# Loads by token halves, contiguous 32x32 turns of rows, and batch 0's query products turned by TensorE for a two-head block matrix, in a new order

## The chip, the cores and the metric

One core of one Trainium2 chip. The metric is the device time of one execution in microseconds (us). Before: a median of 122.04 us over 3 runs (122.0 to 123.68).

## What is computed

Attention with a polynomial sketch, then a small residual network on its output. Cut to what matters:

```python
# q, k, v: (4 batches, 4 heads, 1088 tokens, 32); S1, S2: (8, 32)
def phi(x):                                   # 64 features of a token
    a = np.einsum('rd,bhsd->bhsr', S1, x)
    b = np.einsum('rd,bhsd->bhsr', S2, x)
    return np.einsum('bhsi,bhsj->bhsij', a, b).reshape(*x.shape[:-1], 64)
kv = np.einsum('bhsf,bhsd->bhfd', phi(k), v)
z = np.sum(phi(k), axis=2)
attn = np.einsum('bhsf,bhfd->bhsd', phi(q), kv) / (phi(q) . z + 1e-6)
x = attn.transpose(0, 2, 1, 3).reshape(4, 1088, 128)
xn = (x - mean(x)) / sqrt(var(x) + 1e-6) * g_ln
out = x + relu(xn @ w_ch1) @ w_ch2            # w_ch1 (128, 512), w_ch2 (512, 128)
```

S1, S2 and the two weights arrive as 64-bit words and are turned into float32 on the chip by bit operations (`w_ex` ... `w_mul`, L279 to L341).

## The kernel before

Everything is float32. The four batches go one after another through the attention; each batch gives two chunks of 512 tokens (chunk c = 2b and 2b+1, four tiles of 128) and a rest of 64 tokens, and two rests make the chunks 8 and 9 (one tile each). Each chunk then goes through the network.

**Keys of a batch.** `ld k` brings rows (a partition holds 34 tokens), `turn_g`/`turn_r` (L419, L435) turn them in 32x32 blocks on DVE into kT. Features come in one of two ways: `k_dir` (L461) multiplies nine token tiles of kT with `sk0` and leaves features by token in PSUM, which ACT copies (`k_cp`); or `k_feat` (L478) makes eight small matmuls and `k_tok` (L489) turns their result on DVE. Batches 0 and 1 use the first way, 2 and 3 the second. Then products on POOL or DVE (`k_prod`, `k_prod0`), the sums `k_sum`, `k_zs`, `k_sc`, and `k_val` (72 records on PE) into KV.

**Queries.** Batch 0 is loaded token by token (`ld_t`, `ld_tr`, L149 to L160, runs of 128 bytes) and turned by PE (`turn_p`, L442) with copies on ACT; the others are loaded as rows and turned by DVE. `q_dir` (batch 0) or `q_feat`/`q_tok` give features; `q_ac`, `q_den`, `q_rec`, `q_a2`/`q_b0` make the denominator and scale one factor; `q_prod` makes the 64 products per head and token; `q_turn` (L648) turns them in 32x32 blocks on DVE into qpT; `num` (L656) contracts them with kvr in 32 small matmuls per call (64 records), and `num_cp` copies the result to xT, the chunk by feature.

**Network of a chunk.** `hid` (L770) gives 128 hidden units for 512 tokens in one matmul, `relu` moves them to hT, `sec` (L785) makes one tile of 128 tokens in four matmuls. A chunk's rows for the residual and the statistics come by PE (`row_pe`, chunks 0, 1, 8, 9) or through DRAM (2 to 7): `row_turn` (DVE, L723), `row_wr`, `row_rd` (two DMAs, L729 and L735). `st_bn`, `st_ag` (L748) and `st_pow` (POOL, L756) give the scale, `fin` (DVE) or `fin_a`/`fin_g` (ACT, POOL) the output, `store` the DMA.

PSUM is six tiles: X0 and X1 (two banks each: the letters A, B and C, D of the program), M0 (M), M1 (N), PO (O) and KV (K). The order of everything on every engine is one hand-set table of operations, `PROGRAM` (L840); the framework puts the semaphores between engines by tile, so that a wait may be for a later use of the other half of the same tile. A DMA on SP or ACT is an instruction in that engine's queue; it also waits there until an earlier DMA that used the same of eight semaphores has landed. `fill` (L252) are matmuls on ones that keep PE busy in the opening.

Of the kernel before, what the change touches and what calls it, by code (L numbers as in the profile page):

```python
# [25 lines left out]
def kernel(  # L26
# [121 lines left out]
    @op  # L148
    def ld_t(eng, h, u0, u1):  # L149
        by[eng].dma_start(  # L150
            out=_ap(qt, 0, P, P * u0 + D * h, [[P, u1 - u0], [1, D]]),
            in_=bass.AP(q.tensor, q.offset + (h * S + u0) * D, [[8 * D, P], [D, u1 - u0], [1, D]]),
        )
# [23 lines left out]
    ident8 = const([R, P], F32, "ident8")  # L177
# [264 lines left out]
    def turn_p(z, u0, u1):  # L442
        for u in range(u0, u1):
            n = P if u < 8 else 64
            pe.transpose(banks[z][:, P * (u - u0) : P * (u - u0) + n],
                         qt[0:n, P * u : P * (u + 1)], ident[0:n, 0:n])
# [276 lines left out]
    def row_turn(c):  # L723
        n = tiles(c)
        dve.transpose(_ap(xh[slot(c)], 0, P, 0, [[32 * n, 4], [32, n], [1, 32]]),  # L725
                      _ap(cols(c), 0, P, 0, [[1, 4], [P, n], [4, 32]]))
# [225 lines left out]
```

## Time and profile before

| | |
|---|---|
| median of 3 runs | 122.04 us |
| the profiled execution | 122.71 us, its span 120.9 us |
| PE busy | 108.4 us (90%) |
| DVE busy | 84.0 us (69%) |
| POOL, ACT busy | 48.4 us (40%), 38.7 us (32%) |
| DMA | 15502 packets, 13.31 MB; 6528 packets under 512 bytes |

The span runs from the first to the last recorded instruction; what lies around it (1.81 us in this execution) is start and end of the program. PE is the matmuls, PEld the weight loads beside them; every float32 matmul gives two records. Rows of the timeline read: start, duration of the piece, engine, line, operation, tiles, count, and in brackets the idle time before and what ended it. ACTq and SPq are DMA issues in those engines' queues.

### The profile page before, as it was taken

The page shows a single profiled execution, that of the slowest core. Times are in us where ns is not written, and L with a number is a line of the kernel's source. Part 1 is how long each engine was busy: PE and PEld are TensorE (multiplying, and loading weights), DVE is VectorE, ACT ScalarE, POOL GpSimd, SP SyncE. Part 2 cuts the span into 40 slices and gives each one's busy share as a digit, 9 for nine tenths or more (in the row PEclk, how much of TensorE's full clock was granted, in tenths as well). Part 3 has the DMA queues.
Part 4 walks back from the last instruction along what each step waited for, and adds up shares of the span by engine and source line. Part 5 has one row for each costly group of instructions (what it writes and reads, how often), then busy time and mean ns, then how long its engine had stood idle before and what let it go on. Part 6 is the DMA issues. An engine that isn't in the chain of part 4 may idle for free.

```text
span 120.9 us, 3295 instructions
## 1 busy us (share of the span) xinstructions
PE 108.4 (90%) x1347; PEld 78.6 (65%) x1347; DVE 84.0 (69%) x229; ACT 38.7 (32%) x100; POOL 48.4 (40%) x64
## 2 busy tenths in 40 slices
PE   5993999999898998998999799999979979979970
PEld 3382999848766773874665589766237946549970
DVE  2953308249999799899788999885993655391550
ACT  0062124224334358030701820264491500414000
POOL 6502242035839963301587903339643500006100
PEclk9999999999999999999999999999999999999997
DMA  3999799996000023011640120013640225300423
GB/s 110 262 315 245 139 251 233 272 249 182 0 5 5 0 62 131 0 26 68 203 147 0 43 87 0 5 66 118 188 159 0 87 92 173 91 17 13 161 87 108
DMA packets 15502, 13.31 MB, mean 110 GB/s; under 512 B 6528, under 2 KB 12416, under 8 KB 15488
## 3 DMA queue, kind: packets, MB, share of 16 engines
q1 hardware_dynamic: 11744, 9.54, 28.5%
q10 hardware_dynamic: 3712, 3.57, 9.7%
q8 instruction: 10, 0.16, 0.6%
q14 instruction: 4, 0.03, 0.1%
q0 software_dynamic: 32, 0.00, 0.0%
HBM read 9.31 MB, written 3.80 MB: 108 GB/s over the span
## 4 chain that ended last, share of the span: by engine, by line
PE 57%; DVE 18%; DMA 8%; ACT 6%; issue 4%; POOL 2%; ACTq 1%; DVEq 0%; POOLq 0%
PE X L772 8%; PE M L788 7%; PE X L663 5%; PE M L772 5%; DMA kn<-in_k_dram 4%; PE X L788 4%; DVE xh L725 4%; PE KV L788 3%; PE X L463 3%; DVE qpT L649 3%; DMA w_raw<-in_moe_w_ch_dram 3%; PE PO L788 3%; PE PO L772 2%; ACT xT L82 2%; PE M L463 2%
## 5 line engine op out<-in xcount | busy, mean ns | idle before, releaser
L758 POOL TENSOR_TENSOR rstd<-va,mhalf 128x4 f32<-128x4 f32 (+1 forms) x10 | 10.2, 1024 | 29.1 <-DVE va L752 28.1
L788 PEld LDWEIGHTS M<-w,hT 128*128 128x128 f32 x144 | 17.1, 192 | 5.1 <-issue 2.4
L788 PE MATMUL M<-w,hT 128*128 128x128 f32 x144 | 18.4, 278 | 1.1 <-ACT ob L807 0.6
L772 PE MATMUL X<-xT,w 128*128 128x512 f32 (+1 forms) x38 | 18.4, 586 | 0.8 <-DVE xr L84 0.8
L780 ACT ACTIVATE hT<-X 128x512 f32<-128x512 f32 (+2 forms) x18 | 9.9, 556 | 21.3 <-PE X L772 19.8
L87 POOL TENSOR_TENSOR kp<-kf 128x1280 f32<-128x1280 f32 (+3 forms) x7 | 13.1, 1883 | 4.9 <-ACT kf L82 3.2
L87 POOL TENSOR_TENSOR qp<-a,fq 128x1280 f32<-128x1280 f32 (+1 forms) x4 | 9.6, 2398 | 5.1 <-DVE a L87 5.0
L649 DVE STREAM_TRANSPOSE qpT<-qp 128x1280 f32<-128x1280 f32 (+2 forms) x9 | 11.0, 1227 | 0.5 <-POOL qp L87 0.4
L82 ACT COPY xT<-X 128x256 f32<-128x256 f32 (+1 forms) x13 | 6.1, 510 | 15.9 <-PE X L663 11.5
L772 PE MATMUL M<-xT,w 128*128 128x512 f32 (+1 forms) x20 | 9.0, 532 | 1.4 <-DVE hT L782 0.9
L254 PE MATMUL M<-ones 128*128 128x128 f32 (+2 forms) x16 | 8.7, 696 | 1.4 <-DVE m L202 1.4
L772 PEld LDWEIGHTS X<-xT,w 128*128 128x128 f32 x38 | 6.3, 190 | 4.7 <-issue 4.2
L663 PE MATMUL X<-qpT,kvr 32*32 32x288 f32 (+2 forms) x384 | 7.9, 332 | 1.1 <-issue 0.5
L725 DVE STREAM_TRANSPOSE xh<-xT 128x512 f32<-128x512 f32 x6 | 6.5, 1102 | 0.9 <-ACT xT L82 0.9
L772 PEld LDWEIGHTS M<-xT,w 128*128 128x128 f32 x20 | 3.4, 189 | 5.5 <-issue 1.9
L663 PEld LDWEIGHTS X<-qpT,kvr 32*32 32x32 f32 x384 | 4.7, 103 | 3.0 <-issue 1.0
L745 DVE BATCH_NORM_STATS2 st<-x 128x6 f32<-128x128 f32 x32 | 6.7, 274 | 0.0
L788 PEld LDWEIGHTS X<-w,hT 128*128 128x128 f32 x48 | 5.9, 192 | 1.0 <-issue 1.0
L788 PEld LDWEIGHTS KV<-w,hT 128*128 128x128 f32 x40 | 4.9, 191 | 2.2 <-ACT hT L780 1.7
L788 PE MATMUL X<-w,hT 128*128 128x128 f32 x48 | 6.2, 275 | 0.0
L772 PE MATMUL PO<-xT,w 128*128 128x512 f32 (+1 forms) x14 | 6.2, 522 | 0.0
L817 POOL TENSOR_TENSOR ob<-ob,x 128x512 f32<-128x512 f32 x4 | 5.1, 1282 | 2.5 <-ACT ob L807 2.5
(164 smaller groups left out, 195.2 us busy)
## 6 DMA issues: line engine op xcount, KB each, us to landing
out_dram<-ob SPq DMA_DIRECT2D x7, 256.0 KB, 2.9
vn<-in_v_dram SPq DMA_DIRECT2D x13, 128.0 KB, 4.8
qn<-in_q_dram SPq DMA_DIRECT2D x3, 544.0 KB, 5.6
xd<-xh SPq DMA_DIRECT2D x5, 256.0 KB, 2.3
kn<-in_k_dram ACTq DMA_DIRECT2D x2, 544.0 KB, 6.3
x<-xd SPq DMA_DIRECT2D x4, 256.0 KB, 2.7
kn<-in_k_dram SPq DMA_DIRECT2D x1, 544.0 KB, 7.5
w_raw<-in_moe_w_ch_dram SPq DMA_DIRECT2D x1, 512.0 KB, 6.3
```

What stands on the lines that cost most here:

```text
L82: act.copy(o, i)
L87: by[eng].tensor_tensor(out=o, in0=a, in1=b, op=ALU.mult)
L254: pe.matmul(M[0][:, 0:w], ones[:, 0:P], ones[:, 0:w], start=True, stop=True)
L463: pe.matmul(banks[z][:, KW * (u - u0) : KW * (u - u0 + 1)], kT[b % 2][:, P * u : P * (u + 1)], sk0, start=True, stop=True)
L649: dve.transpose(_ap(qpT, 0, P, 32 * u0, [[32, u1 - u0], [TW, 8], [1, 32]]), qp[:, H * F * u0 : H * F * u1])
L663: pe.matmul(XS[r // 2][D * h : D * h + D, o : o + w], kvr[b % 2][rows, DM * f + D * h : DM * f + D * h + D], qpT[rows, c : c + w], start=( ...
L725: dve.transpose(_ap(xh[slot(c)], 0, P, 0, [[32 * n, 4], [32, n], [1, 32]]), _ap(cols(c), 0, P, 0, [[1, 4], [P, n], [4, 32]]))
L745: dve.bn_stats(out=sts[slot(c)][:, 6 * t : 6 * t + 6], in_=row_ap(c, t))
L758: pool.tensor_tensor(out=rstds[slot(c)][:, 0:n], in0=vas[slot(c)][:, 0:n], in1=mhalf[:, 0:n], op=ALU.pow)
L772: pe.matmul(banks[z][:, 0:n], w1[:, P * j : P * (j + 1)], cols(c)[:, a : a + n], start=True, stop=True)
L780: act.activation(o, i, AF.Relu)
L788: pe.matmul(banks[z][:, DM * t : DM * (t + 1)], h[:, 512 * j + P * t : 512 * j + P * (t + 1)], w2[:, DM * j : DM * (j + 1)], start=(j == 0 ...
```

## The change

* **Loads.** S1 and S2 are stacked on 16 partitions instead of side by side on 8 (`s_raw`, `s_f`, `ident8`); one matmul `sk` gives both columns, and the broadcast for `s2b` becomes an own step, `sk_b`. Batch 0's queries are loaded as rows like the others, in two parts (`ld_h` and `ld`), and turned on DVE by a new `turn_h` (16 tokens of each row, contiguous), which also takes the place of `turn_g` for all queries. `ld_t`, `ld_tr`, `turn_p`, `turn_c` are gone. All early loads but one are issued by SP; ACT issues a single small one.
* **Batch 1's keys** go by `k_feat` and `k_tok` instead of `k_dir` and three copies.
* **Batch 0's numerator.** `q_turn` and `num` are replaced, for batch 0 only, by `q_flip` (PE transposes of 128x128, 18 in all), `q_flcp` (copies of these from PSUM) and `num0`: kv is laid out as a block matrix of two heads (`k_vcp0`, `k_spr0`, `k_rcp0`, kvb cleared by `c_kvb`), and two matmuls per call, each 128 features by 64 outputs, do what 32 small ones did.
* **Rows.** `row_turn` reads a chunk contiguously and writes 32-blocks apart; `row_rd` becomes four DMAs of 32 partitions each; `store` and `store_r` have one layout for all batches.
* **Statistics.** The addition of 1e-6 moves from DVE (`st_ag`) to POOL (`st_pow`).
* **Order.** The whole table is new, with other engines for many copies, relus and products.

The diff, cut to its core:

```diff
-    s_raw = const([R, 2 * D], S1.dtype, "s_raw")
+    s_raw = const([2 * R, D], S1.dtype, "s_raw")
-    qt = const([P, H * TW], F32, "qt")
-    qn = [qt] + const([P, G * D], F32, "qn", B - 1)
+    qn = const([P, G * D], F32, "qn", B)
...
+    def ld_h(eng, x, b, half):
+        ld(eng, x, b, 16 * half, 16 * half + 16)
...
     def sk():
-        for i in range(2):
-            pe.matmul(KV[:, 64 + R * i : 64 + R * (i + 1)], s_f[:, DM * i : DM * (i + 1)],
-                      ident[0:R, 0:R], start=True, stop=True)
-        pe.matmul(KV[:, 80 : 80 + D], ident8, s_f[:, DM : DM + D], start=True, stop=True)
+        pe.matmul(KV[:, 64 : 64 + 2 * R], s_f, ident[0 : 2 * R, 0 : 2 * R], start=True, stop=True)
+    def sk_b():
+        pe.matmul(KV[:, 80 : 80 + D], ident8, s_f[:, 0:D], start=True, stop=True)
...
+    def turn_h(x, b, half):
+        dst, src = turned[x]
+        dve.transpose(
+            _ap(dst[b % 2], 0, P, P * 4 * half, [[32, 4], [P, 4], [1, 32]]),
+            src[b][:, 512 * half : 512 * half + 512],
+        )
...
+    def k_vcp0(eng):
+        copy(eng, _ap(kvc, 0, P, 0, [[F, 2], [1, F]]), _ap(KV, 0, P, 0, [[0, 2], [1, F]]))
+    def k_spr0():
+        pe.transpose(KV[:, 256:384], kvc[:, 0:P], ident)
+    def k_rcp0(eng):
+        for i in range(2):
+            copy(eng, _ap(kvb, 64 * i, 64, 32 * i, [[64, 2], [1, 32]]),
+                 _ap(KV, 64 * i, 64, 256 + 32 * i, [[64, 2], [1, 32]]))
+    def q_flip(u0, u1, p, z):
+        for u in range(u0, u1):
+            pe.transpose(banks[z][:, P * (u - u0) : P * (u - u0 + 1)],
+                         qp[:, 2 * P * u + P * p : 2 * P * u + P * (p + 1)], ident)
+    def q_flcp(eng, u0, u1, p, z):
+        copy(eng, qpT[:, NU * P * p + P * u0 : NU * P * p + P * u1], banks[z][:, 0 : P * (u1 - u0)])
+    def num0(u0, u1, z):
+        for p in range(2):
+            pe.matmul(banks[z][64 * p : 64 * p + 64, 0 : P * (u1 - u0)], kvb[:, 64 * p : 64 * p + 64],
+                      qpT[:, NU * P * p + P * u0 : NU * P * p + P * u1], start=True, stop=True,
+                      tile_position=(0, 64 * p))
...
     def row_turn(c):
         n = tiles(c)
-        dve.transpose(_ap(xh[slot(c)], 0, P, 0, [[32 * n, 4], [32, n], [1, 32]]),
-                      _ap(cols(c), 0, P, 0, [[1, 4], [P, n], [4, 32]]))
+        dve.transpose(_ap(xh[slot(c)], 0, P, 0, [[32, n], [32 * n, 4], [1, 32]]), cols(c))
...
-    def row_rd(eng, c):
+    def row_rd(eng, c, r):
         w = D * tiles(c)
         by[eng].dma_start(
-            out=rows_of(c).rearrange("p (h w) -> p h w", h=H),
-            in_=bass.AP(xd[c].tensor, xd[c].offset, [[w, P], [P * w, H], [1, w]]),
+            out=_ap(rows_of(c), 32 * r, 32, 0, [[w, H], [1, w]]),
+            in_=bass.AP(xd[c].tensor, xd[c].offset + w * r, [[P // 32 * w, 32], [P * w, H], [1, w]]),
         )
...
-        dve.tensor_tensor(out=vas[slot(c)][:, 0:n], in0=_ap(mv, 0, P, 1, [[2, n]]),
-                          in1=eps[:, 0:n], op=ALU.add)
...
     def st_pow(c):
         n = tiles(c)
+        pool.tensor_scalar(out=vas[slot(c)][:, 0:n], in0=_ap(mvs[slot(c)], 0, P, 1, [[2, n]]),
+                           scalar1=1e-6, scalar2=None, op0=ALU.add)
...
     PROGRAM = """
-    c_ones; fill 1 128; ld_g; ld_s S 1; c_pads 1; c_small; c_pads 0; c_vpad 1; c_iota; c_ident;
+    c_ones; fill 1 256; fill 2 512; c_ident; c_iota; ld_s A 1; c_pads 0; ld_g; c_vpad 1;
```

Three places of the order are used by the prediction. Names are tiles (kf features of keys, qt/qp queries and their products, X_65 and X_66 the two-bank PSUM tiles).

ACT from its first instruction to the first copy of key features, before:

```order
L118 DMA kn_73<-in_k_dram 128x512
L165 DMA w_raw<-in_moe_w_ch_dram 128x256
L118 DMA kn_73<-in_k_dram 128x576
L118 DMA kn_74<-in_k_dram 128x1088
L150 DMA qt<-in_q_dram 128x4x32
L206 ACT_TABLE_LOAD
L206 ACTIVATE warm<-one 128x1
L292 ACTIVATE exf_122<-ex_121,m_96 128x256
L150 DMA qt<-in_q_dram 128x4x32
L308 ACTIVATE low_124<-w_raw 128x256
L408 COPY skq_110<-KV 128x16
```

and of the change:

```order
L108 DMA s_raw<-in_S_dram 8x32
L194 ACT_TABLE_LOAD
L194 ACTIVATE warm<-one 128x1
L297 ACTIVATE mant_117<-bits_114,one 16x32
L297 ACTIVATE mant_122<-bits_119,one 128x256
L289 ACTIVATE exf_121<-ex_120,m_95 128x256
L406 COPY skq_109<-KV 128x16
L305 ACTIVATE low_123<-w_raw 128x256
```

Six DMA issues ahead of the copy of the sketch (skq) have become one, and that copy now stands ahead of the weights' low words.

PE from the first key features to batch 0's first query features, before:

```order
L463 MATMUL M_68<-sk_135,kT_103 128x64 x3
L254 MATMUL M_67<-ones 128x128
L463 MATMUL M_67<-sk_135,kT_104 128x64 x3
L463 MATMUL X_66<-sk_135,kT_104 128x64 x3
L505 MATMUL KV<-kf_138 32x32 x9
L445 MATMUL PO<-ident,qt 128x128 x4
L463 MATMUL X_65<-sk_135,kT_104 128x64 x3
L519 MATMUL KV<-zT,s2b 128x32
L254 MATMUL M_67<-ones 128x256
L569 MATMUL PO<-skd_113,qT_105 128x96 x4
```

and of the change, up to the first transposes of products:

```order
L500 MATMUL KV<-kf_137 32x32 x9
L476 MATMUL X_65<-kT_103,sk_135 32x288 x8
L514 MATMUL KV<-zT,s2b 128x32
L356 MATMUL M_67<-w1g,cg 128x256
L564 MATMUL X_66<-skd_112,qT_104 128x96 x4
L500 MATMUL KV<-kf_138 32x32 x9
L564 MATMUL X_66<-skd_112,qT_104 128x96 x5
L514 MATMUL KV<-zT,s2b 128x32
L529 MATMUL KV<-kp,vn_81 32x64 x36
L670 MATMUL M_67<-ident,qp 128x128 x2
```

The nine L463 matmuls of batch 1 and the transposes of qt have left this stretch, eight small L476 matmuls have come in, and both L564 groups (`q_dir 0 4` and `q_dir 4 9`) now write the two halves of one tile, X_66.

ACT around batch 3's numerator, in the change (row_wr is L772, row_rd L778, the chunk's columns xT_156 and xT_157, its rows x_160 to x_163):

```order
L778 DMA x_160<-xd_173 32x4x128 x2
L82 COPY xT_156<-X_65 128x2x128
L778 DMA x_161<-xd_174 32x4x128
L82 COPY xT_157<-X_66 128x2x128
L82 COPY xT_156<-X_66 128x2x128
L778 DMA x_161<-xd_174 32x4x128
L772 DMA xd_176<-xh_167 128x512
L778 DMA x_163<-xd_176 32x4x128
L772 DMA xd_175<-xh_166 128x512
L821 ACTIVATE hT_192<-X_65 128x512
```

Before, the copies of this batch stood on ACT with one store among them and no read or write of rows; now five reads and two writes stand between these copies and the next relu, and the read of x_163 stands right behind the write that it reads.

More of the change, by code (lines that the diff above doesn't have):

```diff
@@ L176 @@
     ident = const([P, P], F32, "ident")
[L177 removed]
+    ident8 = const([2 * R, P], F32, "ident8")
     m8 = const([P, H], F32, "m8")
@@ L859 @@
-    turn_c A N 8 9; k_vcp A 0; turn_c A M 4 8; fold_cp A C 256 512; q_rec 0 0 4; w_e2 V 1 0 256;
-    q_b0 0 4 O 0; k_tok 2; q_prod0 0 2 O 0; w_e3 V 1 0 256; q_turn 0 2; k_spr 0; k_sum 2; k_sc 1;
-    q_dir 4 9 M; k_rcp A 0; num 0 0 2; q_cp A 4 9 M 16 24; num_cp A 0 0 0 2; num_cp A 0 1 0 2;
-    w_add G 1 0 256; c_vpad 2; k_prod G 1 5 9; w_mul G 1 0 256; k_prod G 1 0 5; q_prod0 2 4 O 0;
-    k_sccp V 1; k_zs 2; turn_r q 1; turn_g q 1 0 4; fold O 0 256; k_sc 2; hid N 0 2 0 2;
-    fold_cp A O 0 256; relu A N 0 2 0 2; q_feat 1; q_ac0 4 9 M 4; q_turn 2 4; q_den 0 4 9;
@@ L877 @@
-    q_turn 0 4; relu A C 1 3 0 4; relu A N 0 1 2 4; relu A O 1 2 0 4; row_cp A 1 B;
-    relu A M 1 1 0 4; relu A A 1 0 0 4; sec N 0 3; sec N 0 0; sec N 0 1; num 1 0 9; st_bn 0;
-    turn_g k 3 0 4; turn_r k 3; num_r V 1; num_cp A 1 1 4 8; num_cp A 1 1 0 4; ld_v A 3 3;
-    turn_r q 2; num_cp V 1 0 0 4; num_cp V 1 0 4 8; row_turn 2; row_turn 3; turn_r q 3; st_ag 0;
-    sec N 0 2; sec M 1 3; k_feat 3; k_tok 3; sec M 1 0; hid C 2 1 0 4; k_sum 3; hid O 2 2 0 4;
-    sec M 1 2; row_wr S 3; st_pow 0; fin_a N 0; relu A C 2 1 0 4; row_wr A 2; row_rd S 3;
@@ new lines @@
+    w_e3 V 1 256 512; k_dir 0 6 9 K; k_cp A 0 0 3 N; k_cp A 0 6 9 K; turn_g k 1 0 4;
+    k_prod0 3 5 D 3; turn_r k 1; turn_h q 0 0; sk_qq 2; w_add G 1 256 512; c_pads 1;
+    w_mul G 1 256 512; c_ac 1; k_prod G 0 6 9; sk_qq 3; c_ac 0; k_prod G 0 5 6; fill 1 128;
+    fill 1 256; sk_b; k_sum 0; k_feat 1; k_zs 0; sk_2; k_sc 0; fold M 256 512; k_sccp A 0;
+    q_dir 0 4 C; q_cp A 0 4 C 16 24; turn_h q 0 1; k_tok 1; turn_r q 0; k_sum 1; k_prod0 0 3 N 0;
+    q_ac0 0 4 C 0; w_ex V 1 0 256; q_den 0 0 4; k_zs 1; q_rec 0 0 4; w_bits V 1 0 256;
@@ new lines @@
+    q_flip 4 8 1 N; relu A O 0 1 2 4; q_flcp A 4 8 1 N; hid D 0 0 0 2; hid K 0 3 0 2; num0 4 8 C;
+    k_prod G 1 5 9; turn_g k 2 0 4; hid N 0 1 0 2; w_exf A 2 0 512; relu A K 0 3 0 2;
+    num0_cp A 4 8 C; relu A N 0 1 0 2; relu A M 0 0 2 4; relu V D 0 0 0 2; w_bits V 2 0 512;
+    k_feat 2; q_flip 8 9 1 O; w_low A 2 0 512; q_ac G 1 4 9; q_den 1 4 9; q_ac V 1 0 4;
+    q_den 1 0 4; w_mant V 2 0 512; hid C 1 0 0 4; relu A C 1 0 0 4; q_flcp A 8 9 1 O;
+    hid K 1 1 0 4; row_pe 1 M; k_prod G 1 0 5; w_e2 V 2 0 512; k_tok 2; hid O 1 3 0 4;
@@ new lines @@
+    q_flip 8 9 0 C; hid D 1 2 0 4; row_pe 0 B; w_add G 2 0 512; c_vpad 2; q_rec 1 0 4; q_rec 1 4 9;
+    q_a2 V 1 4 9; w_e3 V 2 0 512; relu V K 1 1 0 4; w_mul G 2 0 512; q_a2 G 1 0 4; row_cp A 1 M;
+    q_flcp A 8 9 0 C; row_cp A 0 B; turn_g k 3 0 4; k_sum 2; k_zs 2; turn_r q 2; st_bn 0;
+    sec N 0 2; sec N 0 3; sec N 0 1; k_sc 2; num0 8 9 N; st_ag 0; turn_h q 2 1; turn_r k 3;
+    k_feat 3; turn_h q 2 0; k_sccp V 2; k_tok 3; k_val 1; num0_r A N; relu A O 1 3 0 4;
+    relu A D 1 2 0 4; k_vcp A 1; q_feat 2; k_sum 3; sec N 0 0; k_spr 1; sec O 1 3; sec O 1 1;
@@ new lines @@
+    relu A N 8 0 0 1; relu A B 3 3 0 4; relu A C 3 2 0 4; relu A K 8 1 0 1; q_turn 0 4;
+    relu V D 8 3 0 1; turn_h q 3 0; relu V M 3 0 0 4; turn_h q 3 1; k_val 2; k_vcp A 2;
+    k_prod V 3 5 9; k_prod G 3 0 5; sec N 3 1; sec N 3 2; k_spr 2; k_sc 3; k_sccp V 3;
+    relu A A 8 2 0 1; sec O 2 3; k_rcp A 2; st_bn 2; q_feat 3; q_tok 3 0; q_tok 3 1; q_ac V 3 0 4;
+    q_den 3 0 4; sec N 3 0; k_val 3; k_vcp A 3; store A 1 0 4; num 2 0 9; q_ac V 3 4 9; st_bn 3;
+    st_bn 8; st_ag 3; st_ag 8; q_den 3 4 9; num_r V 2; sec O 2 2; k_spr 3; num_cp A 2 0 0 4;
@@ new lines @@
+    num_cp A 2 0 4 8; q_rec 3 4 9; num_cp V 2 1 4 8; q_a2 V 3 4 9; num_cp V 2 1 0 4; st_ag 2;
+    st_pow 3; st_pow 2; sec N 3 3; hid C 4 3 0 4; k_rcp A 3; relu A C 4 3 0 4; hid A 4 2 0 4;
+    relu A A 4 2 0 4; fin_a O 2; row_turn 5; row_wr S 5; row_turn 4; store S 0 0 4; row_wr S 4;
+    q_rec 3 0 4; q_prod V 3 4 9; q_turn 4 9; q_a2 V 3 0 4; q_prod V 3 0 4; hid C 5 3 0 4;
+    sec A 8 0; st_pow 8; fin A 8 0; q_turn 0 4; hid D 5 2 0 4; hid B 5 1 0 4; relu A B 5 1 0 4;
+    hid O 5 0 0 4; hid M 4 0 0 4; hid K 4 1 0 4; row_rd S 4 3; fin_g G 2; relu A D 5 2 0 4;
```

204 lines of the change are left out of this document (96 added, 108 removed).

## The prediction

> **What bounds the kernel now.** First the page and the table of stages.
>
> ```profile
> span 120.9 us, 3295 instructions
> PE 108.4 (90%) x1347; PEld 78.6 (65%) x1347; DVE 84.0 (69%) x229; ACT 38.7 (32%) x100; POOL 48.4 (40%) x64
> PE 57%; DVE 18%; DMA 8%; ACT 6%; issue 4%; POOL 2%; ACTq 1%; DVEq 0%; POOLq 0%
> 10.00:20.00 10.00, 8.59 (x56) 8.41 (x56) 3.69 (x12) 2.74 (x9) 3.35 (x10) 1.00 0.96 204
> 30.00:40.00 10.00, 9.13 (x264) 7.13 (x264) 9.82 (x18) 3.95 (x13) 7.42 (x7) 1.00 0.02 4
> 70.00:80.00 10.00, 10.00 (x225) 8.36 (x223) 9.57 (x24) 1.73 (x5) 1.95 (x3) 1.00 0.08 28
> ```
>
> PE is busy in every stage and holds 57% of the chain. DVE is idle for 6.3 of 10 us in the opening and full from 30 on: whoever gives both work sooner shortens the span. Next, the opening and PE's milestones in the timeline.
>
> ```profile
> 6.06 0.39 ACTq L150 DMA_DIRECT2D qt<-in_q_dram  x1
> 9.92 0.41 ACTq L150 DMA_DIRECT2D qt<-in_q_dram  x1
> 10.38 0.43 ACT L308 ACTIVATE low<-w_raw 128x256 f32<-128x256 uint32 x1 [2.00 <-DMA kn<-in_k_dram]
> 10.90 0.19 DVE L401 TENSOR_TENSOR sk<-KV,m 128x32 f32<-128x32 f32 x1 [2.04 <-ACT skq L408]
> 11.41 1.54 PE L463 MATMUL X<-sk,kT 128*128 128x64 f32 x6 [1.86 <-DVE sk L380]
> 33.03 0.68 PE L772 MATMUL M<-xT,w 128*128 128x256 f32 x2
> 91.94 1.60 PE L663 MATMUL X<-qpT,kvr 32*32 32x288 f32 x64
> 116.18 1.06 PE L788 MATMUL X<-w,hT 128*128 128x128 f32 x8
> ```
>
> The first key features (L463) start at 11.41 because ACT, whose copy skq releases DVE, stood behind its own DMA issues, the last at 9.92. The first `hid` starts at 33.03, batch 3's numerator at 91.94, PE ends at 117.24. I follow these milestones.
>
> **The opening.** After, ACT issues one DMA. Keys go first on SP.
>
> ```profile
> kn<-in_k_dram ACTq DMA_DIRECT2D x1, 256.0 KB, 2.8
> 4.87 0.72 POOL L87 TENSOR_TENSOR s_f<-mant,bits 8x256 f32<-8x256 f32 x1 [0.72 <-DVE bits L317]
> 21.37 1.20 PE L254 MATMUL M<-ones 128*128 128x256 f32 x2
> ```
>
> The first piece lands at 0.74 + 2.8 = 3.5, S behind it at 3.6; the turn (0.65), the mask and the small bit operations take DVE to 5.5, s_f to 6.0, `sk` on PE to 6.8. DVE then makes `sk_0` at 7.6, but PE has two fills between (1.1 and 0.6 us at the rate of the row), so `k_dir 0` starts at 8.5: **-2.9**. Bounds: -3.8 if the fills are hidden, -1.5 if S lands 1.4 later, with the first weights.
>
> **Up to the first hid.** Prices of what leaves and comes on PE:
>
> ```profile
> 15.84 1.38 PE L463 MATMUL M<-sk,kT 128*128 128x64 f32 x6
> 18.89 1.12 PE L445 MATMUL PO<-ident,qt 128*128 128x128 f32 x4
> 26.06 1.21 PE L481 MATMUL X<-kT,sk 64*32 64x288 f32 x16
> 54.46 0.72 PE L481 MATMUL X<-kT,sk 64*32 64x288 f32 x16
> 43.30 0.66 PE L715 MATMUL X<-ident,xT 128*128 128x128 f32 x4
> 31.58 0.84 PE L663 MATMUL X<-qpT,kvr 32*32 32x64 f32 x64 [0.42 <-ACT fq L82]
> 18.61 0.69 DVE L87 TENSOR_TENSOR kp<-X,kf 128x512 f32<-128x512 f32 x1 [5.40 <-PE X L463]
> 24.56 0.29 DVE L87 TENSOR_TENSOR ac<-PO,fq 128x128 f32<-128x128 f32 x1 [2.68 <-ACT fq L82]
> 28.16 0.65 DVE L87 TENSOR_TENSOR qp<-PO,a 128x512 f32<-128x512 f32 x1
> ```
>
> Batch 1's `k_dir`, three groups of about 1.2, gives way to `k_feat` at 1.15: -2.5. The nine turns of queries go: -1.9. Batch 2's keys, which PE had done by 33.03 (1.6), now come after the first hid: -1.6. `num 0 0 2` (0.8) and the turn of kv (0.4) go: -1.2. Added: eight `q_flip`, 0.15 each by L715 or 0.28 by L445, in all 1.2 to 2.2, taken 1.7; two `num0` calls, between 0.45 each (the two halves of the array at once) and 0.9 (in turn), with the wait for the copies 1.5 in all; `sk_b` 0.3.
>
> One wait is added. `q_dir 4 9` writes the second half of X1 while DVE still reads `q_dir 0 4`'s result in the first, and must wait for `q_prod0 2 4`; the row at 18.61 shows what such sharing costs now (DVE, 5.40). From the end of `q_dir 0 4`, about 18.9, come ACT's copy (0.3) and DVE's chain from the kind at 24.56 to that at 28.16 (eight operations, 2.4): PE, done with `k_sum 1` at 19.3, stands until 21.65. Queued behind: `q_dir 4 9`, `k_sc 1`, `k_val 0`, the flips. **+2.35**; nothing, if DVE's chain ran 2.4 sooner.
>
> Sum: -2.9 - 2.5 - 1.9 - 1.6 - 1.2 + 1.7 + 1.5 + 0.3 + 2.35 = **-4.3**: first hid at 28.7. Batch 0's copies (ACT to 32% busy) and POOL's products fit beside this.
>
> **From the first hid to the end.** Spacings by row:
>
> ```profile
> 62.58 1.88 PE L772 MATMUL X<-xT,w 128*128 128x512 f32 x4
> 73.14 1.95 PE L788 MATMUL M<-w,hT 128*128 128x128 f32 x16
> ```
>
> One `hid` of 512 columns takes 0.86, one `sec` 0.89. Before, this stretch lasts 84.2 us and holds 32 hid (27.5) and 8 short ones (1.8), 34 sec (30.3), three `k_val` (3.4), three `num` (4.7), the rest of `num 0` (2.0), three `q_feat` (2.1) and small things (3.0): 74.8 of work, so 9.4 of waits and seams. After: batch 2's keys come here (1.1 at this rate), ten flips and five ninths of `num0` (1.2 + 1.5) stand for 2.0: work **+1.8**. The waits I find by following the change's order by hand, engine beside engine, each operation started when its engine and its inputs are free:
>
> * `k_feat 2` behind DVE's turn of batch 2's keys, 0.4;
> * `sec 0` behind w2, whose two last steps now are on POOL behind a product of batch 1, 0.5;
> * `num 1` behind the second `q_turn`, 0.5: POOL makes both products of batch 1 one after the other (2.4 each), and so `num 1` starts near 50.5, hardly before the 50.96 of now; PE has three more `sec` and batch 3's `k_feat` behind it by then;
> * `hid B 3 3` behind the two relus of X0 (the two halves share the wait again), with ACT's four pieces of chunk 1's output ahead of them, 1.1;
> * `k_val 2` behind ACT's relu of chunk 8 in KV, which stands behind two large relus, 1.5;
> * `hid B 5 1` behind `fin A 8 0`, which DVE reaches only after a product of 1024 and before it a turn of 1280, 1.9;
> * the last three chunks, mostly `hid B 7 1` behind DVE's relu of `hid A 6 1` and the short relus at the end, 1.5.
>
> Together 7.4, against 9.4: **-2.0**. Each is uncertain by half; the second, fourth and fifth are ACT's or POOL's order, the others DVE's. Behind each stand all later matmuls, since PE works in order.
>
> DVE's work: what changes by these rows.
>
> ```profile
> L725 DVE STREAM_TRANSPOSE xh<-xT 128x512 f32<-128x512 f32 x6 | 6.5, 1102 | 0.9 <-ACT xT L82 0.9
> L421 DVE STREAM_TRANSPOSE kT<-kn 128x512 f32<-128x512 f32 x2 | 1.3, 681 | 0.0
> L649 DVE STREAM_TRANSPOSE qpT<-qp 128x1280 f32<-128x1280 f32 x4 | 6.0, 1504 | 0.0
> ```
>
> The six turns of rows, 1.10 each, become contiguous like L421: 0.68 (0.42 x 6 = -2.5; nothing, if writing apart costs the same). `q_turn` for batch 0 goes (-2.9), the additions of 1e-6 go to POOL (ten of 0.16, -1.6), w2's last two steps too (-1.4; POOL, at 40%, has room; the small addition there is in no row, between nothing and the 0.72 of s_f, and only a `fin` waits for it); queries' turns (+1.6), `k_tok 1` (+0.8), a `k_prod` of 1280 (+1.5), four more large relus (+1.8) and small ones (+1.0) come: -1.7 of 84. It lies beside PE, and starts earlier; I see its last `q_turn` at 84 where PE wants it at 87. That cover is thin.
>
> **Rows through DRAM.** Six reads become 24.
>
> ```profile
> x<-xd SPq DMA_DIRECT2D x4, 256.0 KB, 2.7
> out_dram<-ob SPq DMA_DIRECT2D x2, 32.0 KB, 1.8
> 102.93 0.60 ACT L780 ACTIVATE hT<-X 128x512 f32<-128x512 f32 x1 [7.37 <-PE X L772]
> ```
>
> A quarter lands in 1.8 to 2.7 us, and each issue takes some 0.4 of its queue: 16 on SP, which has nothing else, 8 on ACT. ACT idles 7.37 in one piece there now; the wait of `row_rd A 7 3` for `row_wr A 7` (about 2.3) holds two relus that PE needs 3 us later. Cost 0; without that cover up to 2.3. Chunk 7's statistics need the rows some 15 us after the numerator, and have them after 8.
>
> **Sum.** -4.3 + 1.8 - 2.0 = -4.5 at PE's end; the tail (a last `fin`, two small stores, 3.6 us) stays. Span 120.9 - 4.5 = 116.4; the profiled execution, 1.8 longer than its span, 118.2; that execution lies 0.67 above the median, so the forecast for a median is 122.04 - 4.5 = **117.5**.
>
> **Rivals.** (1) *The opening runs at the fast rate.* PE works at half rate until about 27:
>
> ```profile
> L254 PEld LDWEIGHTS M<-ones x16: 286/333/337, 1.4 to 21.5; 128*128 128x128 f32 x16
> 28.34 0.42 PEld L445 LDWEIGHTS M<-ident,qt 128*128 128x128 f32 x4
> ```
>
> 333 ns per weight load until 21.5, some 105 at 28.3; L481 takes 1.21 at 26.06 and 0.72 at 54.46. In 4.2 us of fills at the start it did not speed up. The change's fills run unbroken from 1.45 to about 6.2 and on to 8.5. Were PE fast from 8.5, `k_dir` would lose 1.8, `k_feat` 0.5, both `q_dir` 1.5, fold 0.5, flips and fills 1.4; DVE's chain between takes over half of it: -2.5, giving 115.0. Against: the row itself, and the thin L463 stream afterwards.
>
> [...]
>
> (2) *The lead is lost to DVE and POOL.* Operations on DVE beside POOL's long products can take several times their time:
>
> ```profile
> 28.73 2.08 DVE L317 SCALAR_TENSOR_TENSOR bits<-w_raw,ex 128x256 uint32<-128x256 uint32 x1
> 19.22 0.41 DVE L317 SCALAR_TENSOR_TENSOR bits<-w_raw,ex 128x256 uint32<-128x256 uint32 x1
> ```
>
> 1.67 per hit; four on top of those now seen use up the 3 us of cover and put 3.7 on the path: 121.2, no change. For: more of POOL's work now stands beside DVE's. Against: DVE has 7 us more of room early.
>
> (3) *ACT's queue makes it slower.* In the last third five row reads and two writes stand between the copies and relus of batches 2 and 3. Where each waits a whole landing (2.3 to 2.7) on ACT and PE waits for it, a stage loses 2.5. Two such places use up the gain, from three on it is slower by over 2%; four give -4.5 + 10 = +5.5, **127.5**. For: a read right behind its own write on ACT. Against: the 7.37 us that ACT has.
>
> That the change does not do what it says is open for `row_turn`: with 1.10 kept, DVE loses 2.5 of cover; inside the range.
>
> **How the numbers follow.** My forecast 0.54 (116.0 to 119.4); (1) 0.18; (2) 0.21; (3) 0.07. About 2% (2.44 us) is what a measurement of this kernel can tell from no change. Faster by that means below 119.6: 0.54 + 0.18, **0.72**; within, (2): **0.21**; slower **0.07**. The range, with the far ends of the opening (-3.8 and the fast rate) below and (2) above: **114.0 to 121.4**.
>
> **What would show it.** First L463's successor at 8.5 (7.6 to 9.9); a PE gap of about 2 before the second `q_dir`; first hid at 28.7; batch 3's numerator at 87 to 89, not 91.94; rows' turns at 0.68; the late gap behind `fin A 8 0`. Weight loads well under 300 ns before 20 us would mean (1); DVE rows of 1.5 to 2.3 where 0.3 to 0.7 is usual and `num` waiting for `q_turn`, (2); ACTq waits ahead of relus, with PE idle, (3). The forecast is wrong if the numerator of batch 3 starts after 91.

## The result, and the profile after

The changed kernel takes 118.56 us (median of four executions, 117.1 to 123.81); the kernel before, on the same chip, 122.43 (122.0 to 123.68). The ratio is 0.958, with a 95% interval of 0.944 to 0.972: faster. Two of the four executions (119.31 and 123.81, with a lower granted TensorE clock than the others) are left out of the ratio; most of what makes them differ seems to come from this kernel's opening (run 5 below). For a median 117.5 was forecast. The profiled execution took 117.8 us, its span 116.0; forecast were 118.2 and 116.4.

So the end was met. The way to it was not: the milestones of PE stand elsewhere than forecast, and two errors nearly cancel. That the sum came out is luck.

The page of the changed kernel, first lines: span, busy time of the engines, the TensorE clock over 40 slices, and the shares of the chain.

```profile
span 116.0 us, 2979 instructions
PE 101.2 (87%) x1175; PEld 70.8 (61%) x1175; DVE 80.2 (69%) x223; ACT 41.3 (36%) x101; POOL 50.6 (44%) x73
PEclk9999995999999999999999999999999999999999
PE 56%; DVE 26%; DMA 4%; issue 4%; ACT 3%; POOL 1%; SPq 1%; DVEq 0%; POOLq 0%
```

PE lost 7.2 us of work (108.4 to 101.2), and still holds 56% of the chain (57%). One slice of the clock, the seventh (17.4 to 20.3 us), stands near half: a dip that the next rows explain. A 9 ahead of the first dip is no sign of the fast rate: in the kernel before the clock reads 1.00 from 10 to 20 us (the table of stages in the prediction), and three token tiles take 1.54 us there. So the rate is read from durations. PE's milestones in the timeline of the changed kernel (start, duration, engine, line; in brackets the idle time ahead and its releaser):

```profile
1.44 4.63 PE L251 MATMUL M<-ones 128*128 128x256 f32 x6 [1.44 <-DVE ones L185]
6.54 1.18 PE L251 MATMUL M<-ones 128*128 128x256 f32 x4
8.10 0.88 PE L458 MATMUL M<-sk,kT 128*128 128x64 f32 x6 [0.38 <-DVE sk L378]
16.60 1.75 PE L564 MATMUL X<-skd,qT 128*128 128x96 f32 x10 [2.23 <-DVE qp L87]
18.60 2.15 PE L529 MATMUL KV<-kp,vn 128*32 128x64 f32 x72
23.82 1.03 PE L813 MATMUL X<-xT,w 128*128 128x256 f32 x4
46.42 1.60 PE L706 MATMUL X<-qpT,kvr 32*32 32x288 f32 x64
84.50 1.60 PE L706 MATMUL X<-qpT,kvr 32*32 32x288 f32 x64
110.58 1.06 PE L829 MATMUL X<-w,hT 128*128 128x128 f32 x8
```

What to see: the first key features come at 8.10 and take 0.88 us for three token tiles, where the kernel before took 1.54. PE already works at its fast rate. It came to it late in the fills: the first 1280 columns took 4.63 us, 3.6 ns each, the last 384 took 1.18, 3.1 ns each. Then comes the forecast wait of `q_dir 4 9` (2.23), and behind it PE is slow again: `k_val 0` takes 2.15, in the kernel before 1.21. The first `hid` starts at 23.82, 9.2 earlier than before (33.03), where 4.3 were forecast. At the last numerator the lead is 7.4 (84.50 against 91.94; 87 to 89 was forecast), at PE's end 5.6 (111.64 against 117.24). The stretch between the first `hid` and the end of the last `sec`, as one row of the table of windows for each kernel (length, then busy time of PE, weight loads, DVE, ACT, POOL); the kernel before:

```profile
33.03:117.24 84.21, 79.14 (x1047) 55.90 (x1045) 66.11 (x177) 29.52 (x74) 35.96 (x32) 1.00 0.22 73
```

and the changed kernel:

```profile
23.82:111.64 87.82, 81.32 (x973) 56.81 (x971) 64.07 (x169) 31.91 (x77) 40.32 (x38) 1.00 0.26 78
```

It became 3.6 longer: 2.2 more of work and 1.4 more of idle PE (5.1 before, 6.5 now). The largest waits of PE in the changed kernel behind its fills (by line and releaser: us in total, times, longest):

```profile
PE X L564 <- DVE qp L87: 2.2, 1, 2.2
PE X L813 <- DVE hT L823: 1.9, 3, 1.2
PE X L813 <- DVE ob L842: 1.8, 1, 1.8
PE KV L529 <- ACT hT L821: 1.3, 1, 1.3
```

All four are in the forecast's list. The experiments ask three things: what the fast rate in the opening rests on and what it is worth; whether a lead in the opening reaches the end; and whether these waits are order alone.

### The profile page after: what moved, and what is told of

The parts are those of the page before. It is cut to its first block, busy times and chain, and to the rows that moved or that the text cites. A ratio compares the mean times of both kernels' runs of the same rounds, so it can differ in the third digit from the quotient of the medians.

```text
span 116.0 us, 2979 instructions
## 1 busy us (share of the span) xinstructions
PE 101.2 (87%) x1175; PEld 70.8 (61%) x1175; DVE 80.2 (69%) x223; ACT 41.3 (36%) x101; POOL 50.6 (44%) x73
## 4 chain that ended last, share of the span: by engine, by line
PE 56%; DVE 26%; DMA 4%; issue 4%; ACT 3%; POOL 1%; SPq 1%; DVEq 0%; POOLq 0%
PE X L813 9%; PE M L829 9%; PE PO L829 6%; DMA kn<-in_k_dram 4%; PE X L829 4%; DVE qp L87 4%; PE KV L829 4%; PE M L813 4%; DVE hT L823 3%; PE KV L529 3%; PE X L706 3%; PE KV L813 3%; DVE qT L442 2%; PE PO L813 2%; ACT hT L821 2%
## 5 line engine op out<-in xcount | busy, mean ns | idle before, releaser
L829 PE MATMUL M<-w,hT 128*128 128x128 f32 x104 | 13.5, 279 | 0.3
L87 POOL TENSOR_TENSOR kp<-kf 128x1024 f32<-128x1024 f32 (+3 forms) x6 | 10.8, 1796 | 4.7 <-PE KV L529 4.7
L829 PEld LDWEIGHTS PO<-w,hT 128*128 128x128 f32 x72 | 8.8, 191 | 2.3 <-issue 1.9
L829 PE MATMUL PO<-w,hT 128*128 128x128 f32 x72 | 9.7, 280 | 0.2 <-ACT hT L821 0.2
L87 POOL TENSOR_TENSOR qp<-a,fq 128x1024 f32<-128x1024 f32 (+1 forms) x4 | 8.6, 2170 | 0.1
L644 DVE STREAM_TRANSPOSE qpT<-qp 128x1280 f32<-128x1280 f32 (+1 forms) x6 | 8.2, 1359 | 0.4 <-POOL qp L87 0.4
L251 PE MATMUL M<-ones 128*128 128x256 f32 (+2 forms) x16 | 7.1, 577 | 1.4 <-DVE ones L185 1.4
L529 PE MATMUL KV<-kp,vn 128*32 128x64 f32 x288 | 5.8, 244 | 1.3 <-ACT hT L821 1.3
L529 PEld LDWEIGHTS KV<-kp,vn 128*32 128x32 f32 x288 | 5.1, 126 | 2.2 <-ACT hT L821 1.5
L87 DVE TENSOR_TENSOR qp<-a,fq 128x1280 f32<-128x1280 f32 (+1 forms) x3 | 6.3, 2100 | 0.0
```

Source lines behind the costliest of these rows:

```text
L87: by[eng].tensor_tensor(out=o, in0=a, in1=b, op=ALU.mult)
L251: pe.matmul(M[0][:, 0:w], ones[:, 0:P], ones[:, 0:w], start=True, stop=True)
L529: pe.matmul(KV[D * h : D * h + D, 0:F], vn[b][:, TW * h + D * u : TW * h + D * (u + 1)], kp[:, H * F * u + F * h : H * F * u + F * (h + 1) ...
L644: dve.transpose(_ap(qpT, 0, P, 32 * u0, [[32, u1 - u0], [TW, 8], [1, 32]]), qp[:, H * F * u0 : H * F * u1])
L829: pe.matmul(banks[z][:, DM * t : DM * (t + 1)], h[:, 512 * j + P * t : 512 * j + P * (t + 1)], w2[:, DM * j : DM * (j + 1)], start=(j == 0 ...
```

## The experiments

My theory after the result (called A in what follows): PE's fast rate comes from the unbroken fills, PE loses it where it stands idle, and each us won ahead of the first `hid` is won at the end. The rivals: the rate has another source (B); DVE and POOL pace the stretch behind (C). "The ratio" is always to the kernel before on the same chip.

**1. Short fills (e1_short_fills).**

```diff
-c_ones; fill 1 256; fill 2 512;
+c_ones; fill 1 128; fill 1 512;
...
-turn_g k 0 2 4; fill 1 256; fill 1 128; sk_0;
+turn_g k 0 2 4; sk_0;
```

> The changed kernel, whose fills in the opening are cut: 640 columns instead of 1280 ahead of sk and none behind it, so that PE is not kept busy from 1.4 to 7.7 us. Theory A (PE's fast rate after 6.5 us comes from this unbroken run of fills, and a us won ahead of the first hid is worth half a us or more at the end): the first key features (L458) take 1.4 to 1.5 us per three token tiles instead of 0.85, the first hid comes at 26.5 to 28 instead of 23.8, the span is 117.3 to 118.5 instead of 116.0. Rival B (the rate comes from the denser stream behind, not from the fills): L458 stays near 0.85, first hid 23.3 to 24.3, span 115.5 to 116.5. Rival C (the rate is the fills', but the stretch after the first hid is paced by DVE and POOL, so that the lead is worth nothing): first hid 26.5 to 28, span 115.7 to 116.5.

The executions took 122.87, 123.18, 125.17 and 125.22 us; the ratio, from the first two, is 0.999 (0.992 to 1.007). The first is the profiled one, its span 121.1. PE's timeline:

```profile
6.99 1.54 PE L458 MATMUL M<-sk,kT 128*128 128x64 f32 x6 [0.55 <-DVE sk L378]
20.06 2.09 PE L564 MATMUL X<-skd,qT 128*128 128x96 f32 x10 [2.23 <-DVE qp L87]
27.35 1.03 PE L813 MATMUL X<-xT,w 128*128 128x256 f32 x4
84.24 1.12 PE L813 MATMUL X<-xT,w 128*128 128x512 f32 x2 [2.03 <-DVE ob L842]
86.83 1.91 PE L813 MATMUL M<-xT,w 128*128 128x512 f32 x2
115.64 1.06 PE L829 MATMUL X<-w,hT 128*128 128x128 f32 x8
```

The key features take 1.54, so the fills set the rate: B falls. Though they start 1.1 sooner, since no fill is ahead of them, the first `hid` comes 3.5 later. From there to PE's end it takes 89.35, the 87.8 of the changed kernel and 1.5 more: behind the idle 2.03 ahead of `hid 5 1`, `hid` of 512 columns take up to 1.91 instead of 1.02. So the late opening is passed on whole (C falls, on this side), and a second spell of the slow rate comes on top, which puts the span above A's 117.3 to 118.5. Without the fast rate in its opening, and with this spell, the change is worth nothing by this measurement.

**2. Long fills in the kernel before (e2_before_long_fills).** 1792 columns ahead of `sk` instead of 1152, 1280 behind it instead of 640.

```diff
-c_ones; fill 1 128; ld_g;
+c_ones; fill 1 256; ld_g;
...
-fill 2 512; c_masks;
+fill 3 512; c_masks;
...
-fill 1 128; fill 1 256; fill 1 256; k_dir 0 3 6 C;
+fill 1 256; fill 2 512; k_dir 0 3 6 C;
```

> The kernel before with longer fills alone: 1792 columns ahead of sk instead of 1152, 1280 behind it instead of 640; nothing else of the change. Theory A (unbroken fills make PE fast; the lead reaches the end at half or more): L463 takes 0.8 to 0.9 us per three token tiles instead of 1.5, the first hid comes at 29 to 30.5 instead of 33.0, the span is 117.8 to 119.7 instead of 120.9. Rival B (the fills don't set the rate): L463 stays at 1.5, and since the fills then end at 12.6, the first hid comes at 33.5 to 34.5 and the span is 121 to 122.3. Rival C (fast, but ACT's copies and DVE's products set the first hid, or the rest of the kernel takes the lead back): span 120.3 to 121.2.

Ratio 0.994 (0.985 to 1.002), from executions of 121.90 and 122.79 us: no difference that shows. The profiled one is another, of 124.06 (span 122.3). Its timeline:

```profile
11.80 0.88 PE L463 MATMUL X<-sk,kT 128*128 128x64 f32 x6 [1.15 <-DVE sk L380]
14.29 1.38 PE L463 MATMUL M<-sk,kT 128*128 128x64 f32 x6
31.92 0.68 PE L772 MATMUL M<-xT,w 128*128 128x256 f32 x2
```

The fills make PE fast here too, but only for the first nine token tiles; at 14.29 it is slow, and stays so until about 28. The first `hid` gains 1.1, less than A's 2.5 to 4, and this execution loses it again: behind an idle 1.36 ahead of 37.60, PE is slow once more from 37.9 to 41.3. Fills alone don't carry the kernel before: A's size was wrong, since the rate doesn't last. Whether the idle 1.15 or the thin stream of 64-column matmuls ends it, this run doesn't tell.

**3. An own bank for `q_dir 4 9` (e3_q_dir_own_bank).**

```diff
-q_dir 4 9 D;
+q_dir 4 9 O;
...
-q_cp A 4 9 D 0 24;
+q_cp A 4 9 O 0 24;
```

> The changed kernel with q_dir 4 9 in PO, which is free there, instead of the second half of X1, so that it needn't wait for q_prod0 2 4. Theory A (this wait of 2.2 us stands on the path, and the idle PE loses its rate by it): the gap ahead of q_dir 4 9 goes, q_dir 4 9 takes 1.3 instead of 1.75 and k_val 0 1.2 instead of 2.15, the first hid comes at 20.3 to 21.6 instead of 23.8, and the span is 113.8 to 115.3. Rival C (DVE's and POOL's work on batches 1 and 2 sets the stretch behind): the first hid comes as early, but num 1 stays at 45.9 to 46.4 and the span at 115.6 to 116.3. Rival D (the wait only moves to the flips, which need q_prod0 2 4 as well): first hid 22.8 to 23.8, span 115.5 to 116.2.

The executions took 114.17, 119.38, 122.22 and 122.46 us, too far apart for a ratio. The profiled one is that of 122.22:

```profile
9.06 1.03 PE L458 MATMUL M<-sk,kT 128*128 128x64 f32 x6 [1.72 <-DVE sk L378]
9.89 1.49 PE L458 MATMUL X<-sk,kT 128*128 128x64 f32 x6
28.37 1.03 PE L813 MATMUL X<-xT,w 128*128 128x256 f32 x4
```

Here the second half of batch 0's keys landed later; DVE turned it at 8.19 instead of 7.22 and reached `sk_0`, which stands behind that turn, a us later. PE was idle for 1.72 instead of 0.38, and is slow from 9.89 to about 27. The wait ahead of `q_dir 4 9` is gone, as meant, but its price can't be read. What it suggests is that the changed kernel stands on an edge: with the load a us later, the first `hid` starts at 28.37, where run 8, with the same bank and the rate kept, has 20.84. Only this execution is traced; run 5 puts the edge to the test.

**4. An own bank for `sec 8` (e4_sec8_own_bank).**

```diff
-sec A 8 0; st_pow 8; fin A 8 0;
+sec K 8 0; st_pow 8; fin K 8 0;
```

> The changed kernel with sec 8 and fin 8 in KV instead of the first half of X0, so that hid 5 1 needn't wait for DVE's fin 8 (1.82 us of idle PE at 80.9) and hid 4 1, three hid later, does. Theory A (the gap is on the path, nothing else is late there): PE's gap goes, num 3 starts at 82.6 to 83.0 instead of 84.5, the span is 114.1 to 114.8. Rival C (DVE, whose last q_turn ends at 81.97, or POOL's and DVE's rows behind set the end): num 3 at 83 but the span 115.3 to 116.2.

Executions from 116.08 to 120.88; the slower ones aren't traced. The profiled one, the fastest (span 114.3), shows the gap gone and the last numerator 1.7 earlier, at 82.77. From the first `hid` to PE's end:

```profile
24.20:109.90 85.70, 81.04 (x973) 56.98 (x971) 64.06 (x169) 31.95 (x77) 40.33 (x38) 1.00 0.27 80
```

2.1 less than the 87.82 of the changed kernel. A holds: another bank takes this wait away whole.

**5. Longer fills behind `sk` (e5_bridge).** Runs 6 to 9 stand on it.

```diff
-turn_g k 0 2 4; fill 1 256; fill 1 128; sk_0;
+turn_g k 0 2 4; fill 2 512; sk_0;
```

> The changed kernel with 1024 columns of fills behind sk instead of 384, so that PE is busy until the first key features can start, however late the second half of batch 0's keys lands (7.2 to 8.2 us in the traces so far). Theory A (the executions differ by whether PE keeps its fast rate over this wait, 0.4 us in the changed kernel's trace, 1.7 in that of the kernel with q_dir 4 9 in its own bank, which was slow from 9 to 26 us): L458 takes 0.83 to 0.88 and starts at 8.3 to 9.1, first hid at 24 to 24.8, span 116.2 to 117, all executions within 1 us of each other. Rival B (the rate is not set by this idle time): times still spread over 5 us and more, median 118.5 to 121.

Executions of 118.44, 118.45, 118.70 and 119.60; ratio 0.964 (0.958 to 0.971). The spread of 6.7 us has become 1.2 (A said 1). The four later kernels with these fills spread by 1.1 to 2.2, the three without (the changed one, runs 3 and 4) by 4.8 to 8.3. So A's account of the spread holds, from four executions of each: most of it is the idle time ahead of the first key features. The price is 0.7 us (first `hid` at 24.55).

**6. Fills in the wait (e7_fill_wait).** On top of run 5; `fill` gets a bank as an argument.

```diff
-q_prod0 2 4 C 0; q_dir 4 9 D;
+q_prod0 2 4 C 0; fill 2 512 O; fill 1 256 O; q_dir 4 9 D;
```

> The changed kernel with the longer fills behind sk, and 1280 columns of fills (into PO, free there) in the 2.2 us in which PE waits ahead of q_dir 4 9. The wait itself stays. Theory A (the slow work behind this wait, 1.75 for q_dir 4 9 and 2.15 for k_val 0, comes from PE having stood idle): q_dir 4 9 takes 1.25 to 1.35, k_val 0 1.2, first hid 1.2 to 1.7 earlier than with the longer fills behind sk alone, and the span shorter by the same. Rival B (that slowness is k_val's inputs or another load's): both durations and the span stay within 0.4 of it.

Ratio 0.948 (0.941 to 0.954), three of the executions 116.58 to 117.09, against 118.44 to 119.60 in run 5; the fourth, the profiled one, loses as much again to a slow spell behind the idle 2.02 ahead of `hid 5 1` (from there to PE's end 32.5 instead of run 5's 30.8). Here the rows of run 5,

```profile
17.32 1.46 PE L564 MATMUL X<-skd,qT 128*128 128x96 f32 x10 [2.23 <-DVE qp L87]
19.04 2.15 PE L529 MATMUL KV<-kp,vn 128*32 128x64 f32 x72
24.55 1.03 PE L813 MATMUL X<-xT,w 128*128 128x256 f32 x4
```

and those of this one:

```profile
15.01 2.42 PE L251 MATMUL PO<-ones 128*128 128x512 f32 x6
17.31 1.33 PE L564 MATMUL X<-skd,qT 128*128 128x96 f32 x10
18.73 1.21 PE L529 MATMUL KV<-kp,vn 128*32 128x64 f32 x72
23.05 1.03 PE L813 MATMUL X<-xT,w 128*128 128x256 f32 x4
```

`q_dir 4 9` starts at the same time, and nothing else differs; the first `hid` comes 1.5 earlier. So that wait cost 2.2 by itself and 1.5 by the slow rate that it left behind.

**7. Strided turns of rows (e8_strided_turns).** On top of run 5.

```diff
-dve.transpose(_ap(xh[slot(c)], 0, P, 0, [[32, n], [32 * n, 4], [1, 32]]), cols(c))
+dve.transpose(_ap(xh[slot(c)], 0, P, 0, [[32 * n, 4], [32, n], [1, 32]]),
+              _ap(cols(c), 0, P, 0, [[1, 4], [P, n], [4, 32]]))
```

> The changed kernel with the longer fills behind sk, and with the old strided reading and writing in row_turn (six turns; the rows for the residual and the statistics of chunks 2 to 7 then belong to other tokens, so this is not the reference's output; the work is the same in size). Theory A (a strided turn takes 1.10 as before instead of 0.65, 2.5 to 2.7 us of DVE in all, which lie beside PE except ahead of hid 3 3, where DVE's relu releases PE): that gap grows from 1.2 to 2.0, span 0.8 to 1.6 longer than with contiguous turns. Rival C (DVE is the pace of the stretch): span 2 to 3 longer. Rival D (all hidden): within 0.3.

The six turns take 6.3 us, 1060 ns each (678 in the changed kernel). The ratio is 0.963 (0.956 to 0.969), that of run 5 (medians 118.74 and 118.58). The gap ahead of `hid 3 3` is 1.19 in both, so A's gap did not come. The traced execution differs from run 5's in two more ways: it keeps its rate across the wait ahead of `q_dir 4 9` (first `hid` at 23.25), and it loses it for 3.4 us behind `hid 5 1`, which costs the 1.7 that it costs in run 6. Less this, the stretch from the first `hid` to PE's end is 88.2, 0.4 to 0.5 longer than in the changed kernel and in run 5, and `hid 5 1` starts later by as much. D is nearest: on PE's path the contiguous turns are worth 0.5 at most, and by the medians nothing that shows.

**8. Runs 3, 4 and 5 together (e6_all).**

> The changed kernel with the longer fills behind sk, q_dir 4 9 in PO and sec 8 / fin 8 in KV together. Theory A (each wait taken away reaches the end one to one, since the stretch after the first hid is a fixed sequence of 87.8 us on PE, less the 1.8 ahead of hid 5 1): no idle PE from 8.5 to the first hid beyond 0.3, first hid at 20.5 to 21.7, num 3 at 79 to 80.5, span 110.5 to 112.3. Rival C (DVE and POOL set the stretch once PE leads by more): first hid as early, num 1 at 44.5 or later, span 113 to 115.

112.50 us (112.03 to 114.22), ratio 0.912 (0.906 to 0.918), span 110.9. The clock row has no dip but in its last slice, behind PE's end. PE's timeline:

```profile
PEclk9999999999999999999999999999999999999997
```

```profile
16.51 1.21 PE L529 MATMUL KV<-kp,vn 128*32 128x64 f32 x72
20.84 1.03 PE L813 MATMUL X<-xT,w 128*128 128x256 f32 x4
79.35 1.60 PE L706 MATMUL X<-qpT,kvr 32*32 32x288 f32 x64
105.42 1.06 PE L829 MATMUL X<-w,hT 128*128 128x128 f32 x8
```

Against run 5, 3.7 are gained ahead of the first `hid` and 2.1 behind it, and all 5.8 arrive at PE's end (106.48 against 112.27). With a lead of 12 us on the kernel before at the first `hid`, DVE and POOL still don't pace the stretch: C falls on this side too.

**9. Two more waits (e9_two_waits).** On top of run 8.

```diff
-hid B 3 3 0 4; sec O 2 0; hid C 3 2 0 4; hid M 3 0 0 4; sec O 2 1;
+hid O 3 3 0 4; relu A O 3 3 0 4; hid C 3 2 0 4; relu A C 3 2 0 4; hid M 3 0 0 4; sec O 2 0; sec O 2 1;
-relu A B 3 3 0 4; relu A C 3 2 0 4; relu A K 8 1 0 1;
+relu A K 8 1 0 1;
-turn_h q 3 0; relu V M 3 0 0 4;
+relu V M 3 0 0 4; turn_h q 3 0;
```

> The kernel with the longer fills, q_dir 4 9 in PO and sec 8 in KV (span 110.9), and besides: hid 3 3 goes into PO, which is free there, instead of the first X0 half pair, its relu and that of hid 3 2 stand ahead of chunk 8's short relus on ACT, the two sec of chunk 2 stand behind the three hid of chunk 3, and DVE's relu of hid 3 0 goes ahead of a turn of queries. Theory A (the waits ahead of hid 3 3, 1.19, and of k_val 2, 1.34, are only order, and nothing else is late within 2.5 us): both gaps go, num 2 starts 1.8 to 2.5 earlier against the first hid (46.6 behind it now), and the span is 108.3 to 109.3. Rival C (DVE's products beside POOL's are the pace there: k_prod 3 5 9 and 2 0 5 take 2.5 and 3.4 us): k_val 2 or sec 3 1 waits for them instead, num 2 comes 0 to 0.8 earlier, span 110.1 to 111.

110.06 us (109.71 to 110.96), ratio 0.899 (0.890 to 0.908), span 108.2, and so the fastest of all. The stretch:

```profile
20.72:103.76 83.04, 80.73 (x973) 56.92 (x971) 64.07 (x169) 32.05 (x77) 40.45 (x38) 1.00 0.32 92
```

Its idle time on PE is 2.3 us, where the changed kernel has 6.5. Both waits were order alone, at their full size (2.6 gained, 2.5 listed).

**10. ACT's loads on SP in the kernel before (e10_before_sp_loads).** One part of the change alone.

```diff
-ld A k 0 0 16; ld_w A 1 2 4; ld A k 0 16 34; ld A k 1 0 34; ld_t A 2 0 4; ld_t A 3 0 4; ld_v A 0 1;
+ld S k 0 0 16; ld_w S 1 2 4; ld S k 0 16 34; ld S k 1 0 34; ld_t S 2 0 4; ld_t S 3 0 4; ld_v S 0 1;
```

> The kernel before with its seven loads of ACT issued by SP instead, in the same places of the order; nothing else of the change. Theory A (ACT's queue of loads held sk_q and so DVE and the first L463; a lead ahead of the first hid reaches the end one to one): L463 starts at 9.5 to 9.8, when the fills end, instead of 11.41, the first hid comes at 31 to 31.9 instead of 33.0, the span is 119 to 120 instead of 120.9. Rival B (the later chain of ACT's copies, POOL's products and queries' loads sets the first hid): L463 at 9.6, but the first hid at 32.5 or later and the span 120.4 to 121.3.

119.40 us, ratio 0.972 (0.964 to 0.981; whether the gain is over 2% is unclear by this), span 117.6, below A's 119 to 120. PE's timeline:

```profile
9.12 0.88 PE L463 MATMUL X<-sk,kT 128*128 128x64 f32 x6 [1.28 <-DVE sk L380]
11.46 1.27 PE L463 MATMUL M<-sk,kT 128*128 128x64 f32 x6
29.06 0.68 PE L772 MATMUL M<-xT,w 128*128 128x256 f32 x2
112.43 1.06 PE L788 MATMUL X<-w,hT 128*128 128x128 f32 x8
```

The first key features come 2.3 sooner, and at the fast rate for nine token tiles; that saves some 1.7 us more, which I hadn't expected here. The first `hid` comes 4.0 sooner and PE's end 3.75. ACT's queue did hold the opening, as A says. So this one edit, with the rate that it happens to catch, is worth some two thirds of what the whole change is.

## Why the prediction was right at the end and wrong on the way

| | forecast | changed kernel |
|---|---|---|
| first key features | 8.5 | 8.10 |
| from there to the first `hid` | 20.2 | 15.7 (20.4 in run 1) |
| first `hid` | 28.7 | 23.8 |
| first `hid` to PE's end | 84.0 | 87.8 |
| tail | 3.6 | 4.4 |
| span | 116.4 | 116.0 |

**The opening's sum held at the rate it was made for.** Run 1, slow as the forecast assumed (until 17.0 us, and again from 20.4 to 23.8), needs 20.4 from the first key features to the first `hid`, against 20.2. The terms (keys of batch 1 by `k_feat`, queries not turned on PE, flips, `num0`, the wait) add up; they were not measured one by one. `num0` took 0.65 for two tiles, four records of 256 columns, where a `hid` of two such records takes 0.59: the two halves of the array at once. The wait came at 2.23 (2.35 forecast).

**The rate was the first error.** Rival (1) stood at 0.18 and 2.5 us. Its condition came true, and from the first key features to the first `hid` it is worth 4.6 (20.36 less 15.72). I had the 5.7 us of PE time in my own list and struck out more than half, because DVE's chain "takes over". That chain starts only with `q_dir 0 4`; all that PE does ahead of it counts in full. Against the rival I had held 4.2 us of fills that did nothing in one trace, though I had written that the change's fills run on to 8.5 (7.7 it was); that they have only 0.5 us of `sk` inside them, where the kernel before has 1.4, I had not weighed. In every trace here with such fills PE turned fast between about 5 and 7.5 us (the fills behind `sk` took 1.9 to 3.1 ns a column, those ahead of it in the changed kernel 3.6). Even the trace of the kernel before was one draw: in run 10, with the same fills, the six matmuls behind `sk` take 1.35 us instead of 2.50. Why the same fills were enough in one of these two traces and not in the other, no run shows; the fills of run 2 (6.1 us ahead of `sk`) and of the change (4.6, with 1.2 behind it) were enough in every trace of theirs.

**The price of the wait was too low.** 2.35 was forecast for the wait ahead of `q_dir 4 9`; runs 5, 6 and 8 show 3.7, since PE comes out of it slow. Where it doesn't, in run 7's trace, the first `hid` comes 1.3 earlier than in run 5 with the same wait.

**The stretch behind was the second error, and the other way.** "From the first hid to the end" said work +1.8 and waits 7.4 instead of 9.4. The work was right (+2.2), and the list too: `hid B 3 3` 1.1 (1.19), `k_val 2` 1.5 (1.35), `hid B 5 1` 1.9 (1.82), the last chunks 1.5 (1.2); of the three small ones (1.4 together) none came, but 0.5 ahead of a flip did. The failed step is the 9.4. I got it by taking the spacings of the work from the length of the stretch, so that it holds every seam between instructions; the 7.4 is a list of gaps. Like with like, idle PE goes from 5.1 to 6.5: +1.4 where I wrote -2.0. With that, the forecast from my own rows would have been 122.04 - 4.3 + 1.8 + 1.4 = 120.9 at the slow rate; run 1, less its late spell, is at 121.4 (on a chip where the kernel before takes 122.97).

**The tail** is 0.7 longer. Some 0.4 of it is seen: SP is still issuing stores (the row below) and reaches the last small one at 112.53, ACT its own at 112.11.

```profile
110.32 1.70 SPq L863 DMA_DIRECT2D out_dram<-ob  x2
```

**DVE, POOL and ACT.** The turns of rows came out at 0.68, as forecast, but run 7 shows that 0.5 us at most hung on them. The last `q_turn` ends at 82.0 and PE's numerator starts at 84.5: the "thin" cover held (2.5 us; 3 forecast). Rival (2) had its mechanism right, DVE's products of 1280 beside POOL's took 2.70 and 3.44 us, where one without took 1.43, and PE did lose by it, but less than the 3.7: no wait of PE ends at a `q_turn`, with or without 2 us more on DVE. What it cost lies ahead of `hid 5 1`, in the forecast's own list: the `fin 8` that ends this wait stands behind DVE's product of 1024, which took 2.17 beside an addition on POOL, and 1.22 in run 5, where the small product ahead of it takes 1.26 instead of 0.25. So, as an estimate, some 1.0 of the 1.82 is POOL's. Rival (3): a quarter lands in 2.0 us, and no read of rows on ACT held a relu that PE waited for; the read of x_163 is issued at 91.02, the relu behind it starts at 93.38 and waited for PE. As prices of their own both fall. For batch 0's flips, POOL's addition and the quarter reads no run undid the one edit alone; their worth is read from the sum, not shown.
